# One visit per slot for the attention steps 10 to 12, with their sums taken last

## The chip, the cores and the metric

The kernel runs on one core of a Trainium2 chip. The metric is the device time of one execution in microseconds (us). Five engines work side by side, each through its own instructions in order: TensorE (PE, matrix products), VectorE (DVE), ScalarE (ACT), GpSimd (POOL) and SyncE (SP, which here only starts transfers). All data is float32.

## The reference

Attention over 8 batches x 12 heads, 448 positions, head width 64, with q and k normalised by their root mean square; its output, one row of 768 per token, goes through a feed-forward block of width 2048.

```python
q_n, k_n = rmsnorm(q, g_q), rmsnorm(k, g_k)
scores = scale * np.matmul(q_n, k_n.transpose(0, 1, 3, 2))
attn = np.exp(scores - max) ; attn = attn / (sum(attn) + 1e-09)
x = np.matmul(attn, v)            # (B,H,S,D) -> (B*S, H*D)
h = x @ w_in                      # 3584 x 768 @ 768 x 2048
out = (h - np.tanh(h)) @ w_out    # 2048 x 768
```

## The kernel before

**Slots.** The attention is cut into 48 steps of two heads each: step s is the pair of heads s % 6 of batch s // 6. The program is written out in slots, and slot s does step s's values and its division, and the scores of step s+1. Slots -3 to 5 are `first_slot`, 6 to 11 `early_slot`, 12 to 47 `slot`. The feed-forward block of earlier batches is a generator of single matrix products; `run(ns)` takes products from it for a given PE time. So the order on every engine is the order in which this program is written; no planner moves anything. Slots 6 to 8 carry batch 0's first layer (`hidden`, `products`, line 841), slots 9 to 11 its second layer (`project_first`, line 1258, 96 products m = 0 to 95, 32 per slot), slot 12 starts batch 1's first layer.

**One step of attention.** Keys come in four chunks: three of 128 (c = 0, 1, 2) and the last of 64 keys (`KF`). `scores(s, c)` (line 569) puts the scores of the two heads into two PSUM banks, and ACT takes `exp` of each into `p` (chunks 0 and 1), `p_full` (chunk 2) or `p_last` (line 575). `values` (673) and `last_values` (623) multiply by v and accumulate in two banks `av`. `totals` (696) adds the exponentials over the keys by a product with ones into a bank, and DVE takes the reciprocal `rs` (701). `divide` multiplies `av` by `rs` into `xT` (765, four instructions), and for the second half of the heads of batches 0 and 1 POOL forms sums of `xT` for the fast matrix products (`x_sums`, line 793, four instructions). From step 10 on `add`, `add_third`, `add_last` (600, 606, 613) first add the chunks up on DVE, so that `totals` is four matmuls and not sixteen. `turn(s)` transposes the keys and queries of a step on PE through two banks (467, 471), ACT copies them out (469, 475). Squares for the norm are ACT's (132, 133), `norm` is DVE's and POOL's (142 to 144: POOL raises to the power -0.5), and `norm_q` scales q, for steps 9 to 14 on ACT with eight instructions (454), for the others with one on DVE.

**An early slot** has three stops of the attention between products: `totals(s)` and the scores 0 and 1 of s+1 at its start; after a quarter of the slot's products the `turn`; after half of them scores `KF`, the values, the division and scores 2. Then come `add`, `add_last`, `norm` and `norm_q` for later steps, a further eighth of the products ahead of each. From slot 13 (`FOLDED`) on a slot has one visit instead (`visit`, lines 635 and on): scores `KF`, values of chunk 2, then matmuls of scores and values in turns on different rows of the array, the last values, the division, scores 2. There the sums are formed without a bank, on DVE and ACT. Slot 12 has a visit of its own shape: last values, totals, values, then scores 0 to 2 one after the other.

**Banks.** [...]three called `mm` for products, five called `sc`. Each name is handed out in turn (`bank_of`). In slots 6 to 11 all five `sc` are in turn, for scores, totals, turns and `av`; an early slot takes 13. From slot 12 on three are in turn and two are kept for `av`.

**Weights.** In slots 6 to 10 the weights are still being rounded, piece by piece: a transfer into `w_raw` (three buffers, line 293), ACT (71, 72), DVE (78, 79, 82), POOL (92). The transfer of a piece goes into the buffer of the piece three before it, and waits until POOL is through with that. The last four pieces, here called A, B, C and D, are due at m = 29 (end of slot 9), 35, 41 and 47; at a due point ACT's part of that piece is issued, and DVE's and POOL's part of the piece before (at m = 47 of the last two). `combine_w_out` (380 to 383, four DVE instructions) follows from m = 52 on, every four products.

Of the kernel before, what the change touches and what calls it, by code (L numbers as in the profile page):

```python
# [13 lines left out]
ALU = mybir.AluOpType  # L14
# [132 lines left out]
def bounded_path(tc, ctx, q, k, v, moe_w_in, moe_w_out, out, g_col, ident, ones, half_ones, neg_half, early):  # L147
# [18 lines left out]
    B, H, S, D = q.shape  # L166
# [3 lines left out]
    NP = H // 2  # L170
# [7 lines left out]
    HS = S // 2  # L178
# [6 lines left out]
    KF, KR = S // P, S % P  # L185
# [20 lines left out]
    banks = {name: [ps.tile([P, 512], F32, name=f"{name}{i}") for i in range(n)] for name, n in (("sc", 5), ("mm", 3))}  # L206
# [7 lines left out]
    def mm_bank():  # L214
        return bank_of("mm")
# [223 lines left out]
    def squares(s):  # L439
        squares_of(nc, early["sq"], early["n"], loaded["q", s], loaded["k", s])  # L440
# [42 lines left out]
    def by_blocks(s):  # L483
        return has(s) and s >= TURNED
# [67 lines left out]
    def sc_bank():  # L552
        return bank_of("sc")

    def scores(s, c, apart=False):

        rr, kT, qT = turned[s]
        n = S if c < KF else HS
        name, bufs = ("p", 2) if c < 2 else ("p_full", 1) if c < KF else ("p_last", 2)
        if c == 1:  # L560
            p = probs[s, 1] = probs[s, 0]
        else:
            p = probs[s, c] = pp.tile([P, 2, 2 if c < 2 else 1, n], F32, name=name, bufs=bufs)
        tiles = [sc_bank() for _ in range(2)]

        def score(h, i):
            at, first = (i * BL, 0) if c < KF else (i * BL % KR, i * BL // KR * n)
            r = slice(h * D, (h + 1) * D)
            nc.tensor.matmul(  # L569
                tiles[h][i * BL : (i + 1) * BL, :n], lhsT=kT[r, c * P + at : c * P + at + BL],  # L570
                rhs=qT[r, first : first + n], start=True, stop=True,
            )

        def exp(h):
            nc.scalar.activation(  # L575
                p[:, h, c if c < 2 else 0, :], tiles[h][:, :n], AF.Exp,
                scale=1.0 if rr is None else rr[:, 0, 2 * c + h : 2 * c + h + 1],
            )

        if apart:  # L580
            return [(lambda i, h=h: score(h, i), lambda h=h: exp(h)) for h in range(2)]
        for i in range(P // BL):
            for h in range(2):
                score(h, i)
        for h in range(2):
            exp(h)
# [28 lines left out]
    def last_values(s, av):  # L615

        v_nat, p = loaded["v", s], probs[s, KF]
        for n in range(2):
            keys, at = slice(n * KR, (n + 1) * KR), n * HS if s >= FOLDED else 0
            for m in range(2):  # L620
                for h in range(2):
                    r = (2 * m + h) * BL
                    nc.tensor.matmul(  # L623
                        av[n][r : r + BL, at : at + HS], lhsT=v_nat[keys, h, KF, m * BL : (m + 1) * BL],
                        rhs=p[keys, h, 0], start=(s < FOLDED), stop=False, skip_group_check=(s >= FOLDED),
                    )

    def half_values(s, c, av, first):
# [18 lines left out]
    def visit(s, av):  # L647

        wave(*half_values(s, 2, av, True))
        for c in range(2):  # L650
            v0, v1 = half_values(s, c, av, False)
            if has(s + 1):
                (s0, exp0), (s1, exp1) = scores(s + 1, c, True)
                wave(s0, v1)
                exp0()
                wave(v0, s1)
                exp1()
            else:
                wave(v0, v1)
        last_values(s, av)  # L660
        del loaded["v", s]
        divide(s, av)
        if has(s + 1):
            scores(s + 1, 2)

    def values(s, av, chunks=(2, 0, 1)):
        v_nat, p = loaded["v", s], full(s)
# [33 lines left out]
        nc.vector.reciprocal(rs, dn[:, :HS])  # L701


    FOLDED = 2 * NP + 1

    def fold(s):

# [41 lines left out]
    def divide(s, av):  # L749
        b, hp = steps[s]  # L750
        rs = whole.pop(s)
        if b > PAIRED and b % 2 and hp == 1:
            x = xT[b, hp] = late["blocks"].tile([P, S], F32, name="xT_more", bufs=1)
        else:
            x = xT[b, hp] = xp.tile([P, S], F32, name="xT")
        if s >= FOLDED:
            nc.scalar.copy(out=x, in_=av[0][:, :S])
            nc.vector.tensor_tensor(out=x, in0=x, in1=av[1][:, :S], op=ALU.add)  # L758
        for m in range(2):
            rows = slice(m * D, (m + 1) * D)  # L760
            if s >= FOLDED:
                nc.vector.tensor_tensor(out=x[rows], in0=x[rows], in1=rs, op=ALU.mult)  # L762
                continue
            for n in range(2):
                nc.vector.tensor_tensor(
                    out=x[rows, n * HS : (n + 1) * HS], in0=av[n][rows, :HS], in1=rs[n * D : (n + 1) * D],
                    op=ALU.mult,
                )
        for c in range(NCH):
            del probs[s, c]  # L770
        if b < PAIRED and hp >= HC:
            c = hp - HC
            x_sums(b, (c,), range(4), nc.vector if b == 0 and c == HC - 1 else nc.gpsimd)
# [549 lines left out]
    def has(s):  # L1323
        return 0 <= s < NS
# [40 lines left out]

    def early_slot(s):
        gap = gap_ns(s)
        totals(s, sc_bank())
        if has(s + 1):
            scores(s + 1, 0)  # L1370
            scores(s + 1, 1)
        if has(s + 2):
            load(s + 2, "v")
        run(gap)
        if has(s + 2):
            turn(s + 2, sc_bank(), sc_bank())
        if has(s + 3):
            squares(s + 3)
        if has(s + 4) and not by_blocks(s + 4):
            load(s + 4, "qk")  # L1380
        run(gap)
        if has(s + 1):
            scores(s + 1, KF)
        av = [sc_bank() for _ in range(2)]
        last_values(s, av)
        divide(s, values(s, av))
        if has(s + 1):
            scores(s + 1, 2)
        for work, n in ((add, 1), (add_last, 1), (norm, 3), (norm_q, 3)):
            run(gap / 2)  # L1390
            if has(s + n):
                work(s + n)

    def slot(s):

        gap = gap_ns(s)
        av = av_banks
        if has(s + 1):
            scores(s + 1, KF)
        if s < FOLDED:  # L1400
            last_values(s, av)
            totals(s, sc_bank())
            divide(s, values(s, av))
            for c in range(KF):
                scores(s + 1, c)
        else:
            visit(s, av)
        if has(s + 2):
            load(s + 2, "v")
        rows, ahead, following = has(s + 2), has(s + 3), has(s + 1)  # L1410
        folded = following and s + 1 >= FOLDED
        first = s + 3 == TURNED
        scaled = rows and not first
        if scaled:
            power_blocks(s + 2)
        work = (
            (
                (following, lambda: add(s + 1, False)), (first, lambda: turn(s + 2, sc_bank(), sc_bank())),
                (ahead and not first, lambda: load_blocks(s + 3)),
            ),  # L1420
            (
                (following, lambda: add_third(s + 1)), (first, lambda: load_blocks(s + 3)),
                (True, lambda: x_sums_later(s, 0)),
            ),
            ((following, lambda: add_last(s + 1)),),
            ((folded, lambda: fold(s + 1)),),
            ((folded, lambda: fold_rest(s + 1)), (True, lambda: x_sums_later(s, 1))),
            ((scaled, lambda: scale_blocks(s + 2)),),
            ((folded, lambda: gather(s + 1, 0)), (ahead, lambda: square_blocks(s + 3))),
            ((scaled, lambda: turn_blocks(s + 2, 0)), (folded, lambda: gather(s + 1, 1))),  # L1430
            ((scaled, lambda: turn_blocks(s + 2, 1)), (ahead, lambda: norm_blocks(s + 3))),
            ((folded, lambda: spread_sums(s + 1)), (True, lambda: x_sums_later(s, 2))),
            ((scaled, lambda: weigh_keys(s + 2)), (ahead, lambda: meet_blocks(s + 3))),
            ((folded, lambda: widen_sums(s + 1)),),
            ((folded, lambda: turn_sums(s + 1)),),
            (),
        )
        for point in work:
            run(4 * gap / (len(work) + 1))
            for wanted, fn in point:  # L1440
                if wanted:
                    fn()
        run(4 * gap / (len(work) + 1))
# [5 lines left out]
    for s in range(-3, NP):  # L1449
        first_slot(s)  # L1450
    for s in range(NP, 2 * NP):
        early_slot(s)
    banks["sc"], av_banks = banks["sc"][:3], banks["sc"][3:]
    for s in range(2 * NP, NS):
        slot(s)
    run(1e9)
# [345 lines left out]
```

## Time and profile before

| what | us |
|---|---|
| median of 3 runs (1356.78 to 1357.18) | 1356.81 |
| the profiled execution | 1356.19 |
| its span | 1354.4 |
| PE busy | 1317.9 (97%) |
| DVE busy | 949.1 (70%) |
| POOL busy | 775.1 (57%) |
| ACT busy | 556.9 (41%) |

The 1.8 us between the span and the time of the profiled execution lie around the program. Times in views count from the span's start. A line of the timeline is one run of like instructions: start, length, engine, line of the code, operation, tiles, shapes, how many (a float32 matmul shows as two records), and in brackets the time its engine sat idle before it and what ended that. Lengths of neighbouring PE groups overlap, since matmuls are pipelined; the distance from one start to the next is what a group costs. The slots concerned start on PE at 72.96 (slot 6), 109.63, 142.95, 173.10 (slot 9), 206.00 (slot 10), 237.83 and 269.53 (slot 12).

### The profile page before, as it was taken

Reading aid. Unit: us, or ns where it says so; the run is one execution under the profiler, and the core shown is the slowest. Engines: PE = TensorE matmul, PEld = TensorE weight load, DVE = VectorE, ACT = ScalarE, POOL = GpSimd, SP = SyncE. Lnnn points to the kernel's source line nnn. Section 1 sums busy time; section 2 is a strip of 40 time slices with the busy share of each in tenths; the row PEclk is TensorE's granted clock in tenths of the full one; section 3 lists DMA queues with packets and bytes.
Section 4 is the critical chain, followed back from the end, with each engine's and each line's share of the span. In section 5 each row is a group of like instructions: output and inputs, shape, how many; then the busy total and the mean of one; then the engine's idle time right before and its main releaser. Section 6 shows DMA issues by size and latency. Waiting matters only on the chain.

```text
span 1354.4 us, 29206 instructions
## 1 busy us (share of the span) xinstructions
PE 1317.9 (97%) x11336; PEld 1029.0 (76%) x11336; DVE 949.1 (70%) x1393; ACT 556.9 (41%) x1326; POOL 775.1 (57%) x591
## 2 busy tenths in 40 slices
PE   7989999999999999999999999999999999999996
PEld 3467854478998878697778787778787888699985
DVE  4999978757855768587887576768786668434453
ACT  7856654344433454445322446354512264311100
POOL 4766766347846256626698235844699253712761
PEclk9999999999999999999999999999999999999999
DMA  7879889889999667476655867476645775365544
GB/s 172 197 198 266 254 256 254 249 247 280 335 302 274 169 157 182 107 192 151 162 145 138 197 169 179 110 180 163 168 139 139 160 194 158 107 163 178 171 143 84
DMA packets 371688, 253.54 MB, mean 187 GB/s; under 512 B 282196, under 2 KB 310228, under 8 KB 371540
## 3 DMA queue, kind: packets, MB, share of 16 engines
q1 hardware_dynamic: 371536, 251.57, 68.9%
q8 instruction: 92, 1.51, 0.5%
q14 instruction: 56, 0.46, 0.1%
q10 hardware_dynamic: 4, 0.00, 0.0%
HBM read 205.23 MB, written 46.27 MB: 186 GB/s over the span
## 4 chain that ended last, share of the span: by engine, by line
PE 84%; DVE 9%; DMA 2%; SPq 2%; issue 1%; ACT 1%; POOL 1%; DVEq 0%; ACTq 0%
PE mm L841 36%; PE mm L1094 23%; PE sc L569 9%; PE sc L635 6%; PE mm L1258 5%; DVE xT L762 1%; PE sc L673 1%; PE sc L623 1%; SPq L955 1%; PE mm L673 1%; DVE rows L613 1%; DMA w_f<-w_in 1%; DVE rows L606 1%; DVE rows L600 1%; DMA w_f<-w_inner 0%
## 5 line engine op out<-in xcount | busy, mean ns | idle before, releaser
L841 PE MATMUL mm<-xT,w_f 128*128 128x224 f32 x1296 | 264.0, 353 | 0.7 <-DVE s L912 0.7
L841 PEld LDWEIGHTS mm<-xT,w_f 128*128 128x128 f32 x1296 | 244.5, 190 | 6.4 <-issue 4.8
L569 PE MATMUL sc<-qT,kT 64*32 64x448 f32 (+1 forms) x3072 | 214.2, 499 | 2.9 <-ACT p_last L575 1.7
L841 PE MATMUL mm<-tt,w_f 128*128 128x224 f32 x1044 | 213.7, 356 | 0.8 <-DMA w_f<-w_in 0.2
L841 PEld LDWEIGHTS mm<-tt,w_f 128*128 128x128 f32 x1044 | 194.9, 190 | 19.1 <-issue 15.4
L523 POOL TENSOR_TENSOR rr_mine<-rr_mine,neg_half 128x28 f32<-128x28 f32 x33 | 160.6, 4868 | 2.7
L758 DVE TENSOR_TENSOR xT<-xT,sc 128x448 f32<-128x448 f32 x32 | 19.9, 622 | 176.8 <-PE sc L569 119.3
L889 POOL TENSOR_TENSOR gT<-s,th 128x448 f32<-128x448 f32 x44 | 56.1, 1277 | 145.3 <-ACT th L888 142.0
L1094 PE MATMUL mm<-u,w_f 128*128 128x224 f32 x672 | 136.5, 354 | 1.2 <-DVE sum_all L733 0.9
L1094 PE MATMUL mm<-gT,w_f 128*128 128x224 f32 (+1 forms) x480 | 133.0, 429 | 3.1 <-DVE acc L1101 3.0
L1094 PEld LDWEIGHTS mm<-u,w_f 128*128 128x128 f32 x672 | 126.1, 190 | 8.2 <-POOL u L1051 3.9
L569 PEld LDWEIGHTS sc<-qT,kT 64*32 64x32 f32 x3072 | 71.0, 106 | 70.4 <-issue 50.5
L1094 PEld LDWEIGHTS mm<-gT,w_f 128*128 128x128 f32 x480 | 90.2, 190 | 40.7 <-issue 34.2
L635 PE MATMUL sc<-p,v_nat 64*32 64x448 f32 x1120 | 110.5, 536 | 0.0
L1094 PE MATMUL mm<-g,w_f 128*128 128x224 f32 (+1 forms) x360 | 99.5, 428 | 1.1 <-DVE acc L1101 1.1
L725 ACT COPY sum_g<-sum 32x14 f32<-32x14 f32 x280 | 56.3, 201 | 106.1 <-DVE sum L717 100.3
L889 POOL TENSOR_TENSOR g<-s,th 128x448 f32<-128x448 f32 x24 | 30.6, 1278 | 108.2 <-ACT th L888 93.3
L575 ACT ACTIVATE p<-sc 128x448 f32<-128x448 f32 x132 | 71.7, 543 | 50.3 <-PE sc L569 42.4
L1094 PEld LDWEIGHTS mm<-g,w_f 128*128 128x128 f32 x360 | 67.9, 190 | 28.2 <-issue 26.2
L1258 PE MATMUL mm<-gT,w_out 128*128 128x448 f32 x192 | 74.4, 543 | 0.0
L1051 POOL TENSOR_TENSOR u<-gT 128x448 f32<-128x448 f32 x48 | 58.8, 1247 | 11.1 <-PE mm L1094 11.1
L144 POOL TENSOR_TENSOR rr<-rr,neg_half 112x8 f32<-112x8 f32 (+1 forms) x30 | 49.4, 1675 | 26.7 <-DVE rr L143 26.2
(196 smaller groups left out, 2427.9 us busy)
## 6 DMA issues: line engine op xcount, KB each, us to landing
w_f<-w_in SPq DMA_DIRECT2D x196, 384.0 KB, 3.5
w_f<-w_inner SPq DMA_DIRECT2D x63, 512.0 KB, 3.7
w_f<-w_out SPq DMA_DIRECT2D x42, 512.0 KB, 3.9
w_raw<-in_moe_w_out_dram SPq DMA_DIRECT2D x16, 768.0 KB, 5.6
w_in<-w_out SPq DMA_DIRECT2D x21, 384.0 KB, 5.1
qk_nat<-in_q_dram SPq DMA_DIRECT2D x132, 56.0 KB, 2.8
qk_nat<-in_k_dram SPq DMA_DIRECT2D x132, 56.0 KB, 2.3
g<-w_out SPq DMA_DIRECT2D x14, 512.0 KB, 5.1
```

Of the source, the lines that this page charges most:

```text
L144: nc.gpsimd.tensor_tensor(out=r, in0=r, in1=neg_half[:rows], op=ALU.pow)
L523: nc.gpsimd.tensor_tensor(out=mine, in0=mine, in1=neg_half[:, :1].to_broadcast([P, 2 * NJ]), op=ALU.pow)
L569: nc.tensor.matmul(tiles[h][i * BL : (i + 1) * BL, :n], lhsT=kT[r, c * P + at : c * P + at + BL], rhs=qT[r, first : first + n], start=True ...
L575: nc.scalar.activation(p[:, h, c if c < 2 else 0, :], tiles[h][:, :n], AF.Exp, scale=1.0 if rr is None else rr[:, 0, 2 * c + h : 2 * c + h ...
L635: nc.tensor.matmul(av[g][i * BL : (i + 1) * BL, :S], lhsT=v_nat[keys, h, c, m * BL : (m + 1) * BL], rhs=p[keys, h], start=first, stop=True ...
L673: nc.tensor.matmul(av[n][r : r + BL, :HS], lhsT=v_nat[:, h, c, m * BL : (m + 1) * BL], rhs=p[c][:, h, n * HS : (n + 1) * HS], start=False, ...
L725: nc.scalar.copy(out=acc[h * BL : (h + 1) * BL, g], in_=part[g * BL : (g + 1) * BL, h * NJ : (h + 1) * NJ])
L841: nc.tensor.matmul(bank[:, f * HS : (f + 1) * HS], lhsT=w[:, c * width + f, :], rhs=moving[p](c), start=(first and f == 0 and c == 0), sto ...
L889: eng.tensor_tensor(out=g[:, rows, cols], in0=h, in1=th, op=ALU.subtract)
L1051: nc.gpsimd.tensor_tensor(out=u[:, half], in0=a[:, half], in1=z[:, half], op=ALU.subtract)
L1094: nc.tensor.matmul(bank[:, :n], lhsT=w(i), rhs=mv, start=(first and i == 0), stop=(i == len(moving) - 1), skip_group_check=not first,)
L1258: nc.tensor.matmul(bank[:, :S], lhsT=w_out_row(f, n // HC)[:, n % HC * P : (n % HC + 1) * P], rhs=g[:, f, :], start=(f == 0), stop=(f == C ...
```

## The change

Slots 10, 11 and 12 get one visit at their start, in the form that slots from 13 on have, with `av` in two banks kept for it from slot 10 on (`HALVED` = 10), so that three `sc` banks are in turn. The visit ends with scores 2 of the next step; then `totals` in a bank of the products (`mm_bank()`), the reciprocal, and the division, which for these slots first adds the two `av` banks (one ACT copy, one DVE addition) and then multiplies in place. Loads, turn, squares and the four pieces of work at the slot's end keep their places among the products. In slots 6 to 9 one bank of the turn is passed over (`sc_bank()` with no use) ahead of the `turn`, so that its keys no longer go into the bank of `totals` and an early slot takes 14 banks.

```diff
@@ visit(s, av), at its end
         last_values(s, av)
         del loaded["v", s]
-        divide(s, av)
+        if s >= FOLDED:
+            divide(s, av)
         if has(s + 1):
             scores(s + 1, 2)
+        if s < FOLDED:
+            totals(s, mm_bank())
+            divide(s, av)
@@
-    FOLDED = 2 * NP + 1
+    HALVED, FOLDED = 2 * NP - 2, 2 * NP + 1
@@ divide(s, av)
-        if s >= FOLDED:
+        if s >= HALVED:
             nc.scalar.copy(out=x, in_=av[0][:, :S])
             nc.vector.tensor_tensor(out=x, in0=x, in1=av[1][:, :S], op=ALU.add)
...
+                part_of = x[rows, n * HS : (n + 1) * HS]
                 nc.vector.tensor_tensor(
-                    out=x[rows, n * HS : (n + 1) * HS], in0=av[n][rows, :HS], in1=rs[n * D : (n + 1) * D],
-                    op=ALU.mult,
+                    out=part_of, in0=part_of if s >= HALVED else av[n][rows, :HS],
+                    in1=rs[n * D : (n + 1) * D], op=ALU.mult,
                 )
@@ early_slot(s)
-        totals(s, sc_bank())
-        if has(s + 1):
+        if s >= HALVED:
+            scores(s + 1, KF)
+            visit(s, av_banks)
+        else:
+            totals(s, sc_bank())
             scores(s + 1, 0)
             scores(s + 1, 1)
...
         run(gap)
-        if has(s + 2):
-            turn(s + 2, sc_bank(), sc_bank())
+        if s < HALVED:
+            sc_bank()
+        turn(s + 2, sc_bank(), sc_bank())
...
         run(gap)
-        if has(s + 1):
+        if s < HALVED:
             scores(s + 1, KF)
-        av = [sc_bank() for _ in range(2)]
-        last_values(s, av)
-        divide(s, values(s, av))
-        if has(s + 1):
+            av = [sc_bank() for _ in range(2)]
+            last_values(s, av)
+            divide(s, values(s, av))
             scores(s + 1, 2)
@@ slot(s)
-        if s < FOLDED:
-            last_values(s, av)
-            totals(s, sc_bank())
-            divide(s, values(s, av))
-            for c in range(KF):
-                scores(s + 1, c)
-        else:
-            visit(s, av)
+        visit(s, av_banks)
@@ the loop over slots
     for s in range(NP, 2 * NP):
+        if s == HALVED:
+            banks["sc"], av_banks = banks["sc"][:3], banks["sc"][3:]
         early_slot(s)
-    banks["sc"], av_banks = banks["sc"][:3], banks["sc"][3:]
```

More of the change, by code (lines that the diff above doesn't have):

```diff
@@ L618, in last_values @@
         for n in range(2):
-            keys, at = slice(n * KR, (n + 1) * KR), n * HS if s >= FOLDED else 0
+            keys, at = slice(n * KR, (n + 1) * KR), n * HS if s >= HALVED else 0
             for m in range(2):
@@ L624, in last_values @@
                         av[n][r : r + BL, at : at + HS], lhsT=v_nat[keys, h, KF, m * BL : (m + 1) * BL],
-                        rhs=p[keys, h, 0], start=(s < FOLDED), stop=False, skip_group_check=(s >= FOLDED),
+                        rhs=p[keys, h, 0], start=(s < HALVED), stop=False, skip_group_check=(s >= HALVED),
                     )
@@ L1367, in early_slot @@
         gap = gap_ns(s)
-        totals(s, sc_bank())
-        if has(s + 1):
+        if s >= HALVED:
[3 more added lines that the diff above has]
+            totals(s, sc_bank())
             scores(s + 1, 0)
             scores(s + 1, 1)
-        if has(s + 2):
-            load(s + 2, "v")
+        load(s + 2, "v")
         run(gap)
-        if has(s + 2):
-            turn(s + 2, sc_bank(), sc_bank())
-        if has(s + 3):
-            squares(s + 3)
-        if has(s + 4) and not by_blocks(s + 4):
+        if s < HALVED:
+            sc_bank()
+        turn(s + 2, sc_bank(), sc_bank())
+        squares(s + 3)
+        if not by_blocks(s + 4):
             load(s + 4, "qk")
         run(gap)
-        if has(s + 1):
+        if s < HALVED:
             scores(s + 1, KF)
-        av = [sc_bank() for _ in range(2)]
-        last_values(s, av)
-        divide(s, values(s, av))
-        if has(s + 1):
+            av = [sc_bank() for _ in range(2)]
+            last_values(s, av)
+            divide(s, values(s, av))
             scores(s + 1, 2)
@@ L1396, in slot @@
         gap = gap_ns(s)
-        av = av_banks
         if has(s + 1):
             scores(s + 1, KF)
-        if s < FOLDED:
-            last_values(s, av)
-            totals(s, sc_bank())
-            divide(s, values(s, av))
-            for c in range(KF):
-                scores(s + 1, c)
-        else:
-            visit(s, av)
+        visit(s, av_banks)
         if has(s + 2):
```

## The prediction

> **What bounds the kernel now.** I read the page's busy shares and its chain first: PE sets the time, so an edit is worth what it takes from PE's own sequence, and what it adds to PE's waits.
>
> ```profile
> PE 1317.9 (97%) x11336; PEld 1029.0 (76%) x11336; DVE 949.1 (70%) x1393; ACT 556.9 (41%) x1326; POOL 775.1 (57%) x591
> ...
> PE 84%; DVE 9%; DMA 2%; SPq 2%; issue 1%; ACT 1%; POOL 1%; DVEq 0%; ACTq 0%
> ```
>
> Next PE's waits between 58 and 132 us, slots 6 and 7: the two waits for `rs` (slot 6: 1.57 us, slot 7: 2.32) are the turns' keys, which go into the bank of `totals`.
>
> ```profile
> PE sc L467 <- DVE rs L701: 3.9, 2, 2.3
> PE mm L841 <- DVE s L910: 2.5, 1, 2.5
> ```
>
> Then PE's timeline in slot 10: two stops, 206.00 to 208.18 and 221.24 to 225.60, and in slot 13, whose visit (300.78 to 306.21) is the new form.
>
> ```profile
> 206.00 0.58 PE L696 MATMUL sc<-rows,ones 128*32 128x224 f32 x8
> 206.51 1.73 PE L569 MATMUL sc<-qT,kT 64*32 64x448 f32 x32
> 208.18 6.28 PE L1258 MATMUL mm<-gT,w_out 128*128 128x448 f32 x16
> ...
> 221.24 0.61 PE L569 MATMUL sc<-qT,kT 64*32 64x224 f32 x16
> ...
> 225.60 12.29 PE L1258 MATMUL mm<-gT,w_out 128*128 128x448 f32 x32
> ...
> 300.78 0.61 PE L569 MATMUL sc<-qT,kT 64*32 64x224 f32 x16
> 301.19 0.96 PE L635 MATMUL sc<-p_full,v_nat 64*32 64x448 f32 x16
> ...
> 306.21 1.02 PE L841 MATMUL mm<-tt,w_f 128*128 128x224 f32 x4
> ```
>
> Last ACT's timeline at the start of slot 10. ACT is 4.5 us behind PE there: the exponentials of scores whose first matmuls ran at 206.5 start at 210.55, after the weights (which waited for their transfer until 206.48), the copy of y and `norm_q`.
>
> ```profile
> 206.48 0.97 ACT L71 ACTIVATE w_out<-w_raw 128x768 f32<-128x768 f32 x1 [4.89 <-DMA w_raw<-in_moe_w_out_dram]
> 207.36 0.95 ACT L72 ACTIVATE w_raw<-w_raw 128x768 int32<-128x768 uint32 x1
> 208.21 0.50 ACT L1264 COPY s<-mm 128x448 f32<-128x448 f32 x1
> 208.62 2.02 ACT L454 ACTIVATE n<-qk_nat,rr 112x64 f32<-112x64 f32 x8
> 210.55 2.15 ACT L575 ACTIVATE p<-sc,rr 128x448 f32<-128x448 f32 x4
> ```
>
> [...]scores were ready, yet their exponentials stood behind `norm_q`. The forecast goes by the rows. [...]The trace has one case: PE idle for 2.54 us up to 91.28, then from about 91.8 half clock:
>
> ```profile
> 88.00:91.00 3.00, 0.73 (x4) 0.38 (x3) 2.97 (x4) 0.86 (x2) 2.05 (x2) 1.00 1.01 406
> 91.00:93.00 2.00, 1.72 (x6) 1.62 (x7) 1.97 (x3) 0.00 (x0) 1.84 (x2) 0.70 0.11 34
> 93.00:94.00 1.00, 1.00 (x4) 0.50 (x2) 0.97 (x2) 0.00 (x0) 0.00 (x0) 0.50 0.00 0
> ```
>
> The last column but two is the granted clock: 0.70 over 91 to 93 means half clock from 91.8 on. From 94.0 to 95.5 it is 0.59, so half until 95.2. That is 3.4 us at half clock, a loss of 1.7 us of PE work (hidden here, since PE waits for DVE again at 118.5). The waits of 1.57 and 2.32 us had no such sequel. So a PE wait above some 2.5 us may cost 1.7 us more[...].
>
> **The change part by part.**
>
> *Turns of slots 6 to 9: nothing gained.* Slot 6: the turn starts 1.6 us sooner, but DVE has no idle time from 58.9 to 122.1, and PE's next wait (for L910, which DVE ends at 91.2) keeps its end. Slot 7: the turn now waits for the first exponentials, whose banks it takes: ACT is held by `norm_q` until 119.45, the first ends at 120.05, so 0.7 us are won. They are lost at 130.8: scores 2 of that slot (130.44, 1.79 us long where 0.98 is usual) wait for the exponential of `p_last`, which ACT starts at 130.78 after weights that a transfer held. Slot 8: ready in time. Slot 9: ACT's exponentials run from 182.09 and free the new banks at 182.7 and 183.2, the turn stands at 182.53: +0.3 us, and the rest of slot 9 and its weights move with it.
>
> *Stops joined in slots 10 to 12: a gain of 3.4 us before any wait.* Before: 2.18 + 4.36 = 6.54 (slot 10), 237.83 to 240.01 and 253.07 to 257.31 = 6.42 (slot 11), 269.53 to 277.80 = 8.27 (slot 12, where scores 0 to 2 wait for ACT on three banks): 21.2. After: a visit of 5.43 as in slot 13 and `totals` 0.51 (206.00 to 206.51): 5.94 each, 17.8. The turn stays as it is.
>
> *A new wait in each visit, for ACT.* Three banks are in turn. Scores `KF` take two, scores 0 of head 0 the third, and scores 0 of head 1 the first again: they need the first `p_last` exponential. In the visit of slot 13 PE comes to that point 1.91 us after its start (0.41 scores KF, 0.75 values of chunk 2, 0.75 the first mixed wave). Behind the waiting matmul everything on PE stands.
>
> Slot 10: the exponential stands in ACT's queue behind the same rows as before, so it runs at 210.55 and ends at about 210.98; PE is there at 207.9 and goes on at 211.0: 3.1 us. With the 4.05 us left of the visit and `totals` (5.94 - 1.91 = 4.03), PE is through at 215.1.
>
> Slot 12: ACT copies y at the slot's start (269.64, 0.11 after PE), then `norm_q` 2.0, then `p_last` at 271.99: the first ends 2.9 us after the start, PE waits 1.0. This is the least wait while `norm_q` stands there.
>
> Slot 11: here the chain for `norm_q(13)` decides, and it now starts at the end of slot 10's visit, because DVE's and POOL's queues get the division ahead of the weights A to D. From 215.1: `rs` 1.56, addition 0.6, four products 1.6 (218.9); POOL's three `x_sums` that wait for them 3.2 (as 194.44 to 197.65; 222.2); POOL's part of weight A, before at 213.86 with 2.42 (224.6); only then the transfer of D may use A's buffer, 5.8 us from SP's issue at 216.30 to ACT's start at 222.06 (230.4); ACT's L71 0.96, DVE's three on D 2.1 (233.5), transpose of y 0.95, `add` and `add_third` 2.6 (237.0), four combinations 2.1, `add_last` 1.3, four more 2.1 (242.5), `norm`'s first two 0.85, POOL's power 1.7 (245.1), `norm_q` on ACT 2.0, `p_last` 0.4: 247.5. PE: 215.1, eight products 6.1, turn 0.83, 6.1, sixteen 12.25: slot 11 starts at 240.4 and stands at 242.3. Wait: 5.3 us. Before, the same chain ended in time since A's POOL part ran ahead of the division. Its floor is slot 12's 1.0 if the transfer is not on the path; its upper end about 7, with POOL's slowest two (3.68 for 2.42) and the combinations at 2.95.
>
> The sum of waits is 3.1 + 5.3 + 1.0 = 9.4. SP's order does not move; what it waits for is later, but v, q and k have a slot's slack, and weights B, C and D come 2.5 us or more ahead of their products (C: 229.6 against 232.8). Added ACT copies (3 x 0.55) and DVE additions (3 x 0.62) lie behind the visits; `av` and the `mm` bank are free for half a slot. Slot 12's division delays L910 by 0.3 us with 3 to spare.
>
> *Clock.* Slot 11's wait[...]: 0.7 to 1.7 us, taken as 1.2. Slot 10's 3.1[...]: 0 or 1.7, taken as 0.8.
>
> **Sum:** -3.4 + 9.4 + 0.3 + 2.0 = +8.3 us on the profiled 1356.2, so 1364.5; from the median, 0.6 above it, 1365.1. After slot 12 PE shows no wait up to 420 us and 5.9 us of waits from there to the end, mostly for DVE work that follows PE, so next to nothing takes the delay up. Least and most of the unknown terms: slot 11 1.0 to 7, clock 0 to 3.4, so 1358.8 to 1368.2.
>
> **Rivals.** (a) The forecast, 1361.5 to 1368.5: 0.55. (b) The weights' chain is short, since the transfer of D lands early or DVE does its part otherwise: slot 11 waits 1 to 2 us, +2.2 to +3.2 and at most 1.7 for the clock: 1358 to 1361.5; for it speaks that DVE has idle rows of 0.8 and 2.1 us at 217 and 222. 0.2. (c) Faster: the exponential of `p_last` comes before PE needs it. In slot 10 that asks for ACT to be done with `norm_q` by 207.4 rather than 210.55, from which point the gain of 3.4 us decides: 1353.4, range 1351 to 1356. Against it stand the ACT rows, which hang on a transfer and not on PE; 0.12. (d) Weight D or C becomes too late for products m = 54 or 62, or the clock stays low: three to seven more, 1369 to 1374; the slack of 2.5 us speaks against it. 0.1. The rest, 0.03, near no change.
>
> **How the numbers follow.** 1365.1 is (a). The range 1358.0 to 1369.5 takes in (a), (b) and the edge of (d). 0.2% is 2.7 us, about what a measurement of this kernel tells from no change: slower holds (a), (d) and two thirds of (b): 0.78; same a third of (b) and the rest: 0.10; faster (c): 0.12.
>
> **What would show it.** In the new profile PE waits for ACT `p_last` (L575) once in each visit of slots 10 to 12: 3, 5 and 1 us; half clock after the second; no wait of L467 on `rs`, but one of about 4 us on L910 near 87 to 91; PE at slot 12 about 7 us later than 269.53. Wrong it would be if slot 10's visit runs without a wait, or if slot 11's is as short as slot 12's.

## The result and the profile after

The changed kernel takes 1366.66 us (median of 6 runs, 1365.27 to 1368.34); in the same comparison the kernel before takes 1357.37. The ratio is 1.0067, with an interval of 1.0056 to 1.0079: slower by 9.3 us where the prediction had 8.3. The profiled execution took 1366.87 us, with a span of 1365.1.

The page's busy shares and chain answer to the first fence of before. PE has 4.3 us more busy time (slot 11's matmuls at half clock are part of it), ACT 2.7 and DVE 2.3 us more (the three copies and three additions make up 1.6 and 1.7 of these), and DMA, ACT and POOL have each gained a share of the chain.

```profile
PE 1322.2 (97%) x11336; PEld 1030.9 (76%) x11336; DVE 951.4 (70%) x1396; ACT 559.6 (41%) x1329; POOL 776.0 (57%) x591
...
PE 79%; DVE 9%; DMA 4%; ACT 2%; POOL 2%; issue 1%; SPq 1%; DVEq 0%; ACTq 0%
```

PE's waits over the whole span, and then between 200 and 300 us. The 3.9 us of waits for `rs` in the `sc` banks are gone; the wait for L915 (L910 before) has grown from 2.5 to 4.3; and scores wait for `p_last`, 6.6 us of it in slots 10 and 11.

```profile
PE sc L569 <- ACT p_last L575: 7.9, 4, 4.5
...
PE mm L846 <- DVE s L915: 4.3, 1, 4.3
...
PE sc L467 <- ACT p L575: 0.5, 1, 0.5
```

```profile
PE sc L569 <- ACT p_last L575: 6.6, 2, 4.5
```

PE's timeline in slots 10 to 12. The start of a visit (L569 with 64x224, the scores `KF`), the matmul that waits, and the first product behind `totals` are shown.

```profile
206.44 0.61 PE L569 MATMUL sc<-qT,kT 64*32 64x224 f32 x16
...
208.02 1.24 PE L635 MATMUL sc<-p,v_nat 64*32 64x448 f32 x3
211.36 0.56 PE L569 MATMUL sc<-qT,kT 64*32 64x448 f32 x1 [2.10 <-ACT p_last L575]
...
214.91 0.58 PE L700 MATMUL mm<-rows,ones 128*32 128x224 f32 x8
215.42 1.02 PE L1263 MATMUL mm<-gT,w_out 128*128 128x448 f32 x2
...
240.51 0.61 PE L569 MATMUL sc<-qT,kT 64*32 64x224 f32 x16
...
247.82 0.95 PE L569 MATMUL sc<-qT,kT 64*32 64x448 f32 x1 [4.49 <-ACT p_last L575]
...
278.57 0.61 PE L569 MATMUL sc<-qT,kT 64*32 64x224 f32 x16
...
281.50 0.56 PE L569 MATMUL sc<-qT,kT 64*32 64x448 f32 x1
```

Without a wait the matmul comes 1.91 us after the start. Here it comes 4.92 us after it in slot 10, 7.31 in slot 11 and 2.93 in slot 12 (281.50): waits of 3.0, 5.4 and 1.0 us. The brackets show less (slot 12's line has none), since they count from modelled ends. What PE waited for is on ACT. In both slots `norm_q` (L454) runs just ahead of `p_last`; in slot 10 it stood behind a weight and the copy of y, in slot 11 it waited until 245.42 for the norm's last step on POOL (L144):

```profile
208.96 2.02 ACT L454 ACTIVATE n<-qk_nat,rr 112x64 f32<-112x64 f32 x8
210.87 0.77 ACT L575 ACTIVATE p_last<-sc,rr 128x224 f32<-128x224 f32 x2
...
245.42 2.02 ACT L454 ACTIVATE n<-qk_nat,rr 112x64 f32<-112x64 f32 x8 [4.27 <-POOL rr L144]
247.35 0.76 ACT L575 ACTIVATE p_last<-sc,rr 128x224 f32<-128x224 f32 x2
```

In slot 11 each matmul behind the wait lasts 0.95 us and not 0.54. The windows around it give the granted clock in the last column but two: half clock for 3.4 us from the restart.

```profile
246.00:247.80 1.80, 0.00 (x0) 0.00 (x0) 1.37 (x2) 1.80 (x9) 1.80 (x2) 0.97 1.15 330
247.80:249.50 1.70, 1.68 (x23) 0.98 (x31) 0.00 (x0) 0.82 (x2) 0.18 (x1) 0.50 0.79 201
249.50:251.20 1.70, 1.70 (x32) 0.88 (x22) 0.00 (x0) 0.70 (x2) 0.00 (x0) 0.52 1.14 345
251.20:252.00 0.80, 0.80 (x33) 0.52 (x24) 0.00 (x0) 0.57 (x1) 0.00 (x0) 1.00 0.15 42
```

Where the time went, from starts on PE in the two profiles:

| piece | before | after | difference | forecast |
|---|---|---|---|---|
| slots 6 to 9 (start of slot 10) | 206.00 | 206.44 | +0.44 | +0.3 |
| slot 10, its two stops or its visit, with `totals` | 6.54 | 8.98 | +2.44 | +2.5, and 0.8 for the clock |
| slot 11, the same | 6.42 | 12.97 | +6.55 | +4.8, and 1.2 for the clock |
| slot 12, the same | 8.27 | 6.99 | -1.28 | -1.3 |
| turns and products of slots 10 and 11 | | | -0.39 | 0 |
| slots 13 and 14 | | | +1.5 | 0 |
| from there to PE's last group of products | | | -0.3 | 0 |
| behind it (the last stores) | | | +1.7 | 0 |
| span | 1354.4 | 1365.1 | +10.7 | +8.3 |

The forecast had nothing for the last stores, 1.7 us. From DVE's last instruction to the end of the span it is 9.2 us before and 9.3 in the run "turns alone", but 9.9 to 10.9 in the eight kernels that have a joined visit, the changed kernel's 10.9 among them. Each was seen in one execution; what lengthens them was not found.

Slot 11's clock part is 253.48 - 247.82 = 5.66 us from restart to first product, against 4.06 in slot 10: 1.6 us.

### The profile page after: what moved, and what is told of

The parts are those of the page before. It is cut to its first block, busy times and chain, and to the rows that moved or that the text cites. A ratio compares the mean times of both kernels' runs of the same rounds, so it can differ in the third digit from the quotient of the medians.

```text
span 1365.1 us, 29201 instructions
## 1 busy us (share of the span) xinstructions
PE 1322.2 (97%) x11336; PEld 1030.9 (76%) x11336; DVE 951.4 (70%) x1396; ACT 559.6 (41%) x1329; POOL 776.0 (57%) x591
## 4 chain that ended last, share of the span: by engine, by line
PE 79%; DVE 9%; DMA 4%; ACT 2%; POOL 2%; issue 1%; SPq 1%; DVEq 0%; ACTq 0%
PE mm L846 35%; PE mm L1099 23%; PE sc L569 9%; PE sc L635 6%; PE mm L1263 3%; DVE xT L766 1%; PE sc L623 1%; DMA w_f<-w_in 1%; DVE rows L613 1%; DVE rows L600 1%; DMA qk_nat<-in_q_dram 1%; DVE rows L606 1%; PE mm L677 1%; ACT n L454 1%; DVE sum_T L714 1%
## 5 line engine op out<-in xcount | busy, mean ns | idle before, releaser
L569 PE MATMUL sc<-qT,kT 64*32 64x448 f32 (+1 forms) x3072 | 220.1, 502 | 8.6 <-ACT p_last L575 7.9
L569 PEld LDWEIGHTS sc<-qT,kT 64*32 64x32 f32 x3072 | 74.0, 107 | 76.6 <-issue 51.9
L635 PE MATMUL sc<-p,v_nat 64*32 64x448 f32 x1216 | 124.5, 542 | 0.0
L635 PEld LDWEIGHTS sc<-p,v_nat 64*32 64x32 f32 x1216 | 45.2, 108 | 34.0 <-issue 33.8
L144 POOL TENSOR_TENSOR rr<-rr,neg_half 112x8 f32<-112x8 f32 (+1 forms) x30 | 49.3, 1673 | 37.8 <-DVE rr L143 37.3
```

The source lines that it names most:

```text
L144: nc.gpsimd.tensor_tensor(out=r, in0=r, in1=neg_half[:rows], op=ALU.pow)
L569: nc.tensor.matmul(tiles[h][i * BL : (i + 1) * BL, :n], lhsT=kT[r, c * P + at : c * P + at + BL], rhs=qT[r, first : first + n], start=True ...
L635: nc.tensor.matmul(av[g][i * BL : (i + 1) * BL, :S], lhsT=v_nat[keys, h, c, m * BL : (m + 1) * BL], rhs=p[keys, h], start=first, stop=True ...
```

## Experiments

All times are medians; the kernel before stood at 1357.1 in the comparison of the first four runs and at 1356.99 in that of the others. "Offset" is the start of a slot's last values (L623) against the same start in the kernel before.

**Turns alone.** The kernel before, with the skipped bank and nothing else.

```diff
         run(gap)
+        if s < 2 * NP - 2:
+            sc_bank()
         if has(s + 2):
             turn(s + 2, sc_bank(), sc_bank())
```

> Before, with only the turn's bank passed over in slots 6 to 9. Mine: nothing gained, since slots 6 and 7 are held by DVE and then by ACT: within 0.5 us of before, with the wait on L910 about 4.1 us (1.6 us more) and 0.3 us lost at slot 9's turn. Rival, the waits for rs were worth what they show: 1.6 + 2.3 = 3.9 us faster.

Measured: 1356.96, ratio 0.9994 (0.9986 to 1.0002). Its PE waits between 60 and 135 us:

```profile
PE mm L841 <- DVE s L910: 4.3, 1, 4.3
...
PE sc L467 <- ACT p L575: 1.0, 1, 1.0
```

The two waits for `rs`, 3.9 us together, are gone; DVE, which has no idle time there, is where it was, so L910 waits 4.3 us where it waited 2.5. Slot 10 starts at 206.52, 0.5 later, and the offset is +0.40 at slot 13. Nothing is gained, as forecast; the rival of 3.9 us fell.

**Visits alone.** The changed kernel without the skipped bank.

```diff
-        if s < HALVED:
-            sc_bank()
         turn(s + 2, sc_bank(), sc_bank())
```

> The change without the bank passed over in slots 6 to 9, so the visits of slots 10 to 12 alone. Mine: all of the loss is here, 8.5 to 9 us slower than before, with PE waits for p_last of about 3, 5.5 and 1 us. Rival, part of the loss comes from the shifted banks: 2 us or more better than the whole change.

Measured: 1367.87, ratio 1.0071 (1.0058 to 1.0084): the whole loss, 10.8 us where 8.5 to 9 were expected. The first group below is slot 10's restart, the second slot 11's.

```profile
210.76 0.56 PE L569 MATMUL sc<-qT,kT 64*32 64x448 f32 x1 [2.08 <-ACT p_last L575]
...
248.89 0.95 PE L569 MATMUL sc<-qT,kT 64*32 64x448 f32 x1 [4.48 <-ACT p_last L575]
```

Here half clock also fell in slot 10 (a granted clock of 0.70 over 210.6 to 214.0 and 0.77 over 214.0 to 217.0, which is half clock from 212.0 to 215.4), behind a wait of the same 3.0 us that had no such sequel in the changed kernel. Slot 10 took 10.65 us to its products, 1.7 more than in the changed kernel, and slot 11 13.32.

**`norm_q` behind the visit.** The changed kernel, where the eight ACT instructions that scale the queries of steps 12, 13 and 14 are issued right behind the visits of slots 10, 11 and 12, and no longer at the end of the slot before. They read the same data and are due only at the slot's turn.

```diff
             visit(s, av_banks)
+            norm_q(s + 2)
...
             run(gap / 2)
+            if work is norm_q and s + 1 >= HALVED:
+                continue
...
         visit(s, av_banks)
+        if s == 2 * NP:
+            norm_q(s + 2)
```

> The whole change, but norm_q of steps 12, 13 and 14 is issued behind the visit of the next slot, not ahead of it, so that ACT meets the exponentials first. Mine (PE waits because the exponential of p_last stands behind norm_q): slot 10 keeps 1 us of wait for the weight and the copy of y ahead, slots 11 and 12 have none; 10 us less than the whole change, 1 to 2 us faster than before. Rival (the visit itself is slow there, by its mixed matmuls or the sums in a bank of the products): the loss stays within 2 us of the whole change.

Measured: 1356.19, ratio to before 0.9994 (0.9986 to 1.0002), so 10 us less than the change as made. PE's timeline has these lines for the visits of slots 10 and 11, with the first product behind each; slot 12's, from 268.85 to 274.79, is as long as slot 11's:

```profile
205.61 0.61 PE L569 MATMUL sc<-qT,kT 64*32 64x224 f32 x16
...
208.67 0.56 PE L569 MATMUL sc<-qT,kT 64*32 64x448 f32 x1 [0.24 <-ACT p_last L575]
...
212.73 6.28 PE L1263 MATMUL mm<-gT,w_out 128*128 128x448 f32 x16
...
237.82 0.61 PE L569 MATMUL sc<-qT,kT 64*32 64x224 f32 x16
...
243.76 6.28 PE L1263 MATMUL mm<-gT,w_out 128*128 128x448 f32 x16
```

Slot 11 takes 5.94 us, exactly the forecast's figure for a visit with `totals` and no wait, and no clock is lost. ACT's timeline shows why: `p_last` is free of `norm_q`, which runs at 244.86, behind the visit.

```profile
238.86 0.44 ACT L575 ACTIVATE p_last<-sc,rr 128x224 f32<-128x224 f32 x1
...
244.86 2.03 ACT L454 ACTIVATE n<-qk_nat,rr 112x64 f32<-112x64 f32 x8
```

In slot 10 the matmul still comes 3.06 us after the start, a wait of 1.15 (0.24 in the bracket): ahead of `p_last`, ACT has a weight, whose transfer it waits for, and the copy of y.

So the visits themselves cost nothing; the loss is `norm_q` ahead of `p_last` in ACT's queue. A gain over before of 1 to 2 us was expected: of what the joined stops give, PE's last group of products keeps 1.87 us, but the last stores take 1.6 more in the profiled execution, and against before's median 0.9 is left, which this measurement can't tell from nothing.

**D's words elsewhere.** The changed kernel, with the raw words of the last weight piece in an idle slice of another buffer, so that its transfer need not wait for POOL's part of A. It tests the prediction's account of slot 11.

```diff
+        elif n == PIECES - 1:
+            raw = ring[:, 4 * SLOT : 4 * SLOT + 2 * DM].bitcast(I32)
         else:
             raw = wp.tile([P, 2 * DM], I32, name="w_raw", bufs=3)
```

> The whole change, but the raw words of the last weight (D) go into a part of the ring that is idle then, not into A's buffer, so that their transfer does not wait for POOL's part of A. Mine (slot 11's long wait hangs on that transfer): slot 11's wait falls from 5.6 to about 1.2 us and the half clock behind it goes; slot 10 and 12 as they were; 5 to 6 us less than the whole change. Rival (the division ahead in DVE's and POOL's queues makes norm late by itself): slot 11's wait stays above 4 us.

Measured: 1365.94, ratio 1.0064 (1.0049 to 1.008): against before 8.8 us where the change as made has 9.3, not the 5 to 6 us less that the theory asked for. The transfer was issued at 215.82 in place of 225.15, and slot 11's wait is still 4.7 us long. First slot 11's restart; then DVE's timeline of this kernel, with A, B, C and D from 218.81 on and `norm` (L142) at 241.72.

```profile
246.76 0.63 PE L571 MATMUL sc<-qT,kT 64*32 64x448 f32 x1 [3.81 <-ACT p_last L577]
```

```profile
208.86 0.93 DVE L957 STREAM_TRANSPOSE th<-s 128x448 f32<-128x448 f32 x1
215.18 1.56 DVE L707 RECIPROCAL rs<-mm 128x224 f32<-128x224 f32 x1 [5.39 <-PE mm L702]
...
228.93 0.55 DVE L78 TENSOR_SCALAR w_out<-w_out 128x768 f32<-128x768 f32 x1
229.51 1.25 DVE L79 TENSOR_SCALAR w_out<-w_out 128x768 int32<-128x768 int32 x1
230.80 1.65 DVE L82 SCALAR_TENSOR_TENSOR w_out<-w_f,w_out 128x768 int32<-128x768 int32 x1
...
241.72 0.68 DVE L142 TENSOR_REDUCE rr<-n 112x8 f32<-112x512 f32 x1
```

DVE has no idle time between 215.18 and `norm`. With the transfer early, DVE's own queue is the path: the reciprocal holds it for 5.39 us until `totals` is there, then it has the division, four pieces of weights in 13.6 us, the transpose of y, the additions and eight combinations ahead of `norm`. Below stand, first, the reciprocal and the first instruction on A in the kernel before, where the reciprocal had nothing to wait for, and then, from the changed kernel, the reciprocal, the first instructions on A and on D, and `norm`:

```profile
209.85 1.56 DVE L701 RECIPROCAL rs<-sc 128x224 f32<-128x224 f32 x1
211.33 0.50 DVE L78 TENSOR_SCALAR w_out<-w_out 128x768 f32<-128x768 f32 x1
```

```profile
215.56 1.56 DVE L705 RECIPROCAL rs<-mm 128x224 f32<-128x224 f32 x1 [5.32 <-PE mm L700]
...
219.19 0.56 DVE L78 TENSOR_SCALAR w_out<-w_out 128x768 f32<-128x768 f32 x1
...
230.81 1.11 DVE L78 TENSOR_SCALAR w_out<-w_out 128x768 f32<-128x768 f32 x1 [1.44 <-ACT w_out L71]
...
242.78 0.68 DVE L142 TENSOR_REDUCE rr<-n 112x8 f32<-112x512 f32 x1
```

In the changed kernel DVE did wait for D, 1.44 us, so there the transfer's path ended last. But counted from the reciprocal, `norm` comes after 27.22 us there and after 26.54 here: the queue's own path ended only 0.7 us earlier, and 0.7 us is what slot 11's wait lost. The theory that the transfer makes that wait fell.

**`norm` ahead of the additions.** The changed kernel with another order of the pieces at the end of slots 10 and 11, so that DVE meets `norm` before the additions and combinations. It tests whether the queue is the path.

```diff
-        for work, n in ((add, 1), (add_last, 1), (norm, 3), (norm_q, 3)):
+        order = ((add, 1), (add_last, 1), (norm, 3), (norm_q, 3))
+        if s >= HALVED:
+            order = ((norm, 3), (add, 1), (add_last, 1), (norm_q, 3))
+        for work, n in order:
```

> The whole change, but in slots 10 and 11 norm is issued ahead of add, so that four additions and eight combinations of weights no longer stand ahead of it in DVE's queue. Mine, as it is after the run with D elsewhere (slot 11's wait hangs on how late DVE's queue comes to norm): norm starts near 234.5, power and norm_q follow in time, slot 11's wait falls from 5.4 to about 1.2 us and its half clock goes: 5 to 6 us less than the whole change, 3 to 4 us slower than before. Rival (ACT or POOL is late by itself there): slot 11's wait stays above 4 us.

Measured: 1360.96, ratio 1.0029 (1.0022 to 1.0036): 4.0 us over before, 5.3 less than the change as made. The DVE line, then ACT's:

```profile
234.79 0.63 DVE L142 TENSOR_REDUCE rr<-n 112x8 f32<-112x512 f32 x1
```

```profile
241.11 0.53 ACT L1269 COPY s<-mm 128x448 f32<-128x448 f32 x1 [8.71 <-PE mm L1263]
241.54 2.02 ACT L454 ACTIVATE n<-qk_nat,rr 112x64 f32<-112x64 f32 x8
243.46 0.76 ACT L575 ACTIVATE p_last<-sc,rr 128x224 f32<-128x224 f32 x2
```

`norm` is 8 us earlier, `norm_q` starts right behind the copy of y, and slot 11 takes 241.00 to 248.00: 7.0 us, the same as slot 12, with no half clock. That is the floor the prediction gave, a wait of 1.0, and here D's transfer still waits for POOL's part of A, as in the changed kernel.

**Slot 12 alone.** Only slot 12 in the new form: banks parted behind the early slots, no skipped bank.

```diff
-    HALVED, FOLDED = 2 * NP - 2, 2 * NP + 1
+    HALVED, FOLDED = 2 * NP, 2 * NP + 1
...
```

> Before, with the visit in slot 12 alone, no bank passed over. Mine: PE's stop in slot 12 falls from 8.3 to 7.0 us with one wait of 1 us for p_last: 1.3 us faster. Rival (a joined visit loses wherever it stands): slower than before.

Measured: 1356.11, ratio 0.9994 (0.9987 to 1.0). Slot 12 takes 269.36 to 276.36, 7.0 us in place of 8.27, and the offset is -1.44 at slot 13 and -1.40 at slot 15 (the profiled execution, at 1358.46 the slowest of twenty, loses it again near the end). The mechanism is as forecast; the median moved by 0.9 where 1.3 were expected, and the interval ends at 1, so this measurement hardly tells it from nothing.

**`norm_q` behind the visit, no skipped bank.** The kernel with `norm_q` later, without the two lines of the skip.

> As norm_q later, without the bank passed over in slots 6 to 9. Mine: 0.3 to 0.4 us less than with it, 2 us faster than before; no wait of slot 9's turn for an exponential. Rival (the bank passed over is worth something once the visits don't wait): 1 us or more slower than with it.

Measured: 1356.59, ratio 0.9992 (0.9983 to 1.0), offset -1.49 at slot 13; the 2 us over before that were expected are not there. Against the run with the skip no difference can be told, as the two intervals show: the turns' part stays unsettled below half a us.

**Scores `KF` ahead.** The last kernel, with the scores `KF` of step 11 issued four products ahead of slot 10's start, so that ACT has time for their exponentials.

```diff
+            if work is norm_q and s + 1 == HALVED:
+                part_banks()
+                scores(s + 2, KF)
             run(gap / 2)
...
```

> As norm_q later without the bank passed over, and scores KF of step 11 stand four products ahead of slot 10, so that ACT takes their exponentials ahead of the weight and the copy of y. Mine: the last wait for p_last in slot 10, 1.2 us, goes, against 0.2 us for one more change between products and scores: 2.5 to 3 us faster than before. Rival (ACT is late in slot 10 anyway, for the next exponentials): no better than without it.

Measured: 1356.0, ratio 0.999 (0.9983 to 0.9996). No visit of slots 10 to 12 waits for `p_last`; products follow at 212.36 and 243.39. One more change between products and scores cost about 0.3 us, an estimate from starts on PE: the scores `KF` ahead of the slot take 0.54 (203.05 to 203.59) where a visit's take 0.41, and the four products behind them 3.20 where half of eight take 3.06 (215.12 to 221.24 in the kernel before). Its ratio is the lowest of all and the only one whose interval lies wholly below 1, though the intervals overlap, and the gain is 1 us where 2.5 to 3 were expected: the offset of -2.46 at slot 13 shrinks to -1.94 and then -1.04 further on.

## Why the prediction was right, and where it was not

- *Turns of slots 6 to 9, nothing gained:* right. Alone they gave a ratio of 0.9994, and DVE's wait took over what `rs` gave back (2.5 to 4.3). Slot 7's gain went at 131.54, as forecast at 130.8; slot 10 starts 0.44 later (forecast 0.3).
- *Stops joined, -3.4:* right. A visit with `totals` and no wait takes 5.94 us (slot 11 with `norm_q` later), the forecast's own figure.
- *Wait in slot 10, 3.1:* 3.0, with the restart at 211.36 where 211.0 was forecast from a start 0.44 earlier. The cause is shown in the main: with `norm_q` out of ACT's way 1.15 of it is left, and with the scores `KF` ahead nothing.
- *Wait in slot 12, 1.0:* 1.0.
- *Wait in slot 11, 5.3:* the size is right (5.4), and the chain that the prediction named did run: D on ACT 229.88 against 230.4, `norm` reached at 242.78 against 242.5, restart 247.82 against 247.5. The step that failed is "here the chain for `norm_q(13)` decides", where it runs over POOL's part of A and "only then the transfer of D": it does not decide alone. With that transfer 9.3 us earlier the wait shrank by only 0.7. DVE's queue holds `norm` back nearly as long, and the prediction counted that queue only from D on. A, B and C were in it as well, from 219.19 to 229.38, with 2.8 us for A, 3.9 for B and 3.5 for C, where the prediction took 2.1 for D. That the number came out although this path was left out is luck: the path ended 0.7 us before the one that was counted. The prediction asked what the transfer waits for, and not what would stand there if it waited for nothing.
- *"Its floor is slot 12's 1.0 if the transfer is not on the path":* the floor is right and the condition wrong. With the transfer off the path the wait was 4.7; an earlier `norm` in DVE's queue reached the floor with the transfer still in its place.
- *Clock:* slot 11 1.6 (forecast 1.2), slot 10 none (0.8). In visits alone slot 10 paid as well, so a mean of 0.8 was fair, but it is one or the other. Of the forecast's 0.7 to 1.7 for slot 11 the upper end is half of the 3.4 us in the trace of before; the lower end follows from no row and was the author's estimate. The bound "above some 2.5 us", in waits as the brackets show them, rested on one case and did not hold: behind a bracket of 2.08 in visits alone half clock came. Beside the turns, half clock of 6.8 us (90.8 to 97.6) cost nothing, since PE waits again in slot 7 (0.50 us for ACT at 120.41).
- *"PE at slot 12 about 7 us later":* this figure didn't follow from the prediction's own terms, which give 0.3 + 2.5 + 0.8 + 4.8 + 1.2 = 9.6. Measured: 9.04.
- *"Next to nothing takes the delay up":* right for the end (offset +8.98 at PE's last group, +7.76 at slot 13), but 1.5 us more were lost in slots 13 and 14. PE's waits between 300 and 420 us, of which before had none there, are these two:

```profile
PE mm L846 <- DMA w_f<-w_in: 0.5, 1, 0.5
PE mm L846 <- DVE s L922: 0.2, 1, 0.2
```

  By starts on PE, as above, the wait for the transfer costs 0.74 us in slot 14 and the other 0.40 in slot 13. The last 0.4, in smaller pieces of slot 13, was not traced.

- *Rivals:* (c), faster, is what the kernel would have been with ACT's queue in another order; even then it is 1 us and not 3.4. Slots 13 to 17 give part of the gain back (-2.09 becomes -1.44 with `norm_q` behind the visit), and what is left is near what can be measured. (b) fell by the length of slot 11's wait, and (d) since no product waited for weights there.

One term is only argued: the reciprocal's hold on DVE's queue, 5.3 us of idle time. Had it stood behind the weights, only A could have filled that time, since ACT had done its part of A by then (from 206.86) and began B at 216.58. That is about 2.1 to 2.8 us by the durations above, an estimate; no kernel was run with that order.

## What to carry to other kernels

When scores and values are merged into one visit with fewer banks, the first exponential can become PE's pacemaker (PE waited 3.0, 5.4 and 1.0 us for it here): list what stands ahead of it in ACT's queue at that moment, and move behind the visit whatever isn't due yet. Here that alone was worth 10 us, while the merge itself is worth about 1, near the least that was told from no change. When a wait is put down to one long path, work out the second one too (what the engine's own queue holds if that path were instant); two paths that end within 1 us look alike in one trace, and only a run that removes one of them tells which to mend.

## What the runs showed of the hardware

- **Half clock came in stretches of 3.4 or 6.8 us, and a wait of 3.0 to 3.1 us brought one in one kernel and none in three.** Slot 10's wait brought none in the changed kernel (a granted clock of 1.00 in the 4 us behind it), and none with D elsewhere or with `norm` ahead (the matmuls behind it last 0.54 to 0.56 us there, and not the 0.95 of half clock), but 3.4 us in visits alone. Slot 11's wait brought 3.4 us in the changed kernel, matmuls of 0.95 us with D elsewhere too, and 6.8 us in visits alone (a granted clock of 0.77 over 243.0 to 248.8, 0.50 to 252.2 and 0.89 to 255.7, begun while PE still stood). The wait of 4.3 us for L915 in the changed kernel went with 6.8 us too (0.50 over 90.8 to 94.2, 0.51 to 97.6), that of 2.5 for L910 in the kernel before with 3.4. What decides whether a wait brings it was not shown: no run here moved a wait alone.
- **DVE's rounding was slower beside POOL's part of a piece (L92).** Two DVE instructions of the same shape in the changed kernel, with POOL idle at 231.95 and at work (226.07 to 228.56) at 226.44:

```profile
226.44 1.25 DVE L79 TENSOR_SCALAR w_out<-w_out 128x768 int32<-128x768 int32 x1
...
231.95 0.56 DVE L79 TENSOR_SCALAR w_out<-w_out 128x768 int32<-128x768 int32 x1
```

  L82 goes from 0.96 to 1.65 us likewise: 0.69 us more each. Beside other work of POOL's it was less or nothing: L79 and L82 take 0.90 and 1.30 us at 219.78 beside `x_sums` (L798), but 0.56 and 0.96 at 207.84 beside the norm's power (L144, 206.62 to 209.90). Why is not shown. The slowing made a piece of weights cost up to 3.9 us rather than 2.1 (as at 207.25 to 209.31) just where four of them stood in a row.
